# Batch 0's attention in products of 512 columns, with E and F loaded as 128 rows and the first half of k loaded uncast

## The chip, the cores and the metric

The kernel runs on one core of one Trainium2 chip. The metric is the device time of one execution in microseconds (us), the median over runs. The kernel before has 320.8 us (three runs, 320.7 to 321.04).

## The reference

Eight batches of attention with projected keys and values feed a maxout layer and an output product:

```python
k_proj = einsum('ks,bhsd->bhkd', E, k)          # E, F: 64 x 1024
v_proj = einsum('ks,bhsd->bhkd', F, v)          # q, k, v: 8 batches x 8 heads x 1024 x 64
attn = softmax(q @ k_proj^T / 8)                # 1024 x 64 for each head
x = (attn @ v_proj), heads side by side         # 8192 x 512
out = maximum(x @ w1, x @ w2) @ w_out           # 512 -> 1024 -> 512
```

Inputs and output are float32; the kernel computes in float16 with float32 accumulation.

## The kernel before

Every step is a Python function that issues instructions, and the order of the calls is the order on each engine: the schedule is written out by hand. Names in the profile are tile names; `step_...` are the functions.

The kernel has a short opening stage (0 to about 27 us) and a long steady stage. The opening stage loads and computes the attention of batch 0 and starts its first layer; the steady stage interleaves the attention of batch b + 1 with the two layers of batch b.

**Loads.** Three loads go on the SP queue: E (64 rows of 1024 float32), the first two heads of k as float32 (`kf_sb`, cast later by ScalarE and VectorE), and F. All others go on the POOL queue and are cast to float16 on the way: k heads 2 and 3; q heads 0 to 3; k heads 4 to 7; q heads 4 to 7; v in four pairs of heads; then the weights, in pieces. The first four pieces of the weights are the first 256 columns of w2 and w1: rows "g = 0" of w2, of w1, rows "g = 1" of w2, of w1. In what follows the fourth is called w1g1; POOL issues it at 16.04 us. From the ninth load of the POOL queue on, each waits until the one eight places earlier has landed.

**Attention of batch 0.** It goes in two groups of four heads (g = 0, 1) and, within a group, two halves of 256 query columns each (j = 0, 1).

- `step_eft(i)` transposes E and F by float32 transposes (L161); one copy evacuates each (L167).
- `step_kv(..., "k")` projects k for four heads (L187), `step_kpt` transposes the result (L277), `step_qt` transposes q (L303).
- `step_sc(g, j)` makes the scores (L332: tiles of 64 rows by 32 columns, 256 columns of q) and ScalarE takes the exponential (L372). `step_dn` sums by a product with ones (L344) and takes the logarithm (L380), `step_inv` the exponential of its negative (L384), that is the reciprocal.
- `step_kv(..., "v")` projects v, once for each half of the partitions, since the values are wanted on both.
- `step_at(g, j)` multiplies with the values (L344), and VectorE scales with the reciprocal into `xt_sb` (L399), two instructions for each (g, j), one for each output half o.

**First layer of batch 0.** `step_wd(f0, r0, r1)` (L495, VectorE) forms `wd = w1 - w2` for 256 columns and the row blocks r0 to r1. `up_slots` (L479) multiplies `xt` with `wd`, four row blocks r for each output block. The first four output blocks, two of each j, take r = 0, 1 as soon as group 0 is done, and r = 2, 3 when group 1 is. `step_w2t(f0)` (L504) transposes w2 for a later use. With its second argument it takes a buffer of the ring `att`.

**PSUM.** `mm_bank()` gives one of four banks in the order of the list `turn`; `att_banks()` gives the next of a ring of two buffers of two banks. A new user of a buffer waits for the last reader of the old one. Fillers, `warm(n)` (L147), are products of ones that nobody reads.

The end of the opening stage, as the calls are written:

```python
    step_kv(t, 4, 8, "v", True, copy=nc.scalar.copy)
    step_at(t, 1, 0, True)
    u0, u1 = [*up_slots(t, 0)], [*up_slots(t, 1)]
    step_wd(0, 2, 4)
    step_at(t, 1, 1, True)
    for u in u0, u1:
        for x in u[0:2]:
            x(r1=2)
    step_w2t(0, True)
```

After this come, for TensorE, `u0[0]` and `u0[1]` with r = 2, 3, `step_w2t(256, True)`, `u1[0]` and `u1[1]` with r = 2, 3, and the rest of the layer. The buffers of the ring `att` there: `step_at(1, 0)` has one, `step_at(1, 1)` the other, `step_w2t(0)` the first of the two again, `step_w2t(256)` the second.

Of the kernel before, what the change touches and what calls it, by code (L numbers as in the profile page):

```python
# [16 lines left out]
def kernel(  # L17
# [55 lines left out]
    def big(n, dtype=FP16):  # L73
        return const.tile([128, 16384 // mybir.dt.size(dtype) // 2], dtype, tag=f"big{n}", name=f"big{n}")

    ef_sb = big(0, FP32)[0:KP, :].rearrange("k (i s) -> k i s", i=2)
    kf_sb = const.tile([128, 2048], FP32, tag="wo", name="kf_sb")[:, 0 : 2 * NC * D].rearrange(
        "p (h c d) -> p h c d", h=2, d=D
    )
    nc.sync.dma_start(out=ef_sb[:, 0, :], in_=E)  # L80
    nc.sync.dma_start(out=kf_sb, in_=k[0, 0:2].rearrange("h (p c) d -> p h c d", c=NC))
    nc.sync.dma_start(out=ef_sb[:, 1, :], in_=F)
# [27 lines left out]
    for h0 in (0, H // 2):  # L110
        for n, src in (("k", k), ("q", q)):
            load(tiles[0], n, src, 0, h0 + 2 * ((h0, n) == (0, "k")), h0 + H // 2)
            if (h0, n) == (0, "k"):
                ident = const.tile([128, 128], FP32)
                make_identity(nc, ident)
# [24 lines left out]
    nc.vector.memset(ones16, 1.0)  # L140
    junk = const.tile([1, 1], FP16)


    def warm(n, att=False):
        w_ps = att_banks()[:, 0, :] if att else mm_bank()
        for _ in range(n):
            nc.tensor.matmul(  # L147
                out=w_ps, lhsT=ones16[:, 0:128], rhs=ones16, start=True, stop=True
            )

    warm(8)
    ident16 = const.tile([128, 128], FP16)
    nc.vector.tensor_copy(out=ident16, in_=ident)


    eft = [const.tile([128, NC, KP], FP16, tag=f"eft{i}", name=f"eft{i}") for i in range(2)]

    def step_eft(i):
        eft_ps = mm_bank()
        for c in range(NC):  # L160
            nc.tensor.transpose(  # L161
                out=eft_ps[:, c * KP : (c + 1) * KP],
                in_=ef_sb[:, i].rearrange("k (p c) -> k c p", c=NC)[:, c, :],
                identity=ident[:KP, :KP],
            )
        eng = nc.scalar.copy if i else nc.vector.tensor_copy
        eng(out=eft[i].rearrange("p c k -> p (c k)"), in_=eft_ps)  # L167
# [9 lines left out]
    def step_kv(t, h0=0, h1=H, which="kv", att=False, dma=False, copy=nc.vector.tensor_copy):  # L177
        kv_ps = att_banks()[:, 0, :] if att else mm_bank(n=0 if dma else None)
        n = (h1 - h0) * D
        both = which == "v"  # L180
        nh = 2 if both else h1 - h0
        for h in range(0, h1 - h0, nh):
            for c in range(NC):
                for w in which:
                    i = "kv".index(w)
                    for r in range(2) if both else (i,):
                        nc.tensor.matmul(  # L187
                            out=kv_ps[r * KP : (r + 1) * KP, h * D : (h + nh) * D],
                            lhsT=eft[i][:, c, :],
                            rhs=t[w][:, h0 + h : h0 + h + nh, c, :],  # L190
                            start=(c == 0), stop=(c == NC - 1),
                        )
        zd = lambda ap: ap.rearrange("p (h d z) -> p h z d", d=D // 2, z=2)
        if "k" in which:
            eng = nc.vector.tensor_copy if which == "k" or dma else nc.scalar.copy
            kp = t["kp"][:, h0:h1]
            eng(out=kp[:, :, 0, :], in_=kv_ps[0:KP, 0:n].rearrange("p (h d) -> p h d", d=D))
        if both:
            copy(out=t["vp"][:, h0:h1], in_=zd(kv_ps[:, 0:n]))
        elif "v" in which:  # L200
            def finish_v():
                nc.vector.tensor_copy(out=t["vp"][KP:128, h0:h1], in_=zd(kv_ps[KP:128, 0:n]))
                if dma:
                    nc.vector.tensor_copy(out=kp[:, :, 1, :], in_=kp[:, :, 0, :])
                    step_kpt_dma(t)
                else:
                    step_vp(t, h0, h1)

            if att:
                return finish_v  # L210
            finish_v()
# [59 lines left out]


    def step_kpt(t, h0=0, h1=H, att=False):
        kpt_ps = att_banks(FP16)[:, 0, :] if att else mm_bank(FP16)
        for h in range(h0, h1):
            for r in range(2):
                nc.tensor.transpose(  # L277
                    out=kpt_ps[r * D : (r + 1) * D, (h - h0) * KP : (h - h0 + 1) * KP],
                    in_=t["kp"][:, h, 0, :],
                    identity=ident16[:KP, :KP],  # L280
                )
        nc.vector.tensor_copy(
            out=t["kpt"][:, h0:h1, :].rearrange("q h k -> q (h k)"),
            in_=kpt_ps[:, 0 : (h1 - h0) * KP],
        )
# [100 lines left out]
    def step_at(t, g, j, att=False, between=None):  # L386
# [9 lines left out]
        for o in range(2):  # L396
# [7 lines left out]
            )  # L404

# [121 lines left out]
    T_sb = const.tile([128, 4, NG + NX, CH], FP16)  # L527
# [35 lines left out]
    def m_steps():  # L563
# [41 lines left out]
        def p5():  # L605
            st["s5"] = keep("pu", product(5, "Z", 3))
# [333 lines left out]
    for u in u0, u1:  # L940
        for x in u[0:2]:
            x(r1=2)
# [203 lines left out]
```

## Time and profile before

| | |
|---|---|
| median of the runs | 320.8 us |
| time of the profiled execution | 321.09 us |
| its span, first to last instruction | 319.3 us |
| TensorE (PE) busy | 312.9 us, 98% |
| VectorE (DVE) busy | 241.3 us, 76% |
| ScalarE (ACT) busy | 205.8 us, 64% |
| GpSimd (POOL) busy | 39.7 us, 12% |
| granted TensorE clock | 1.000 |

Busy time is a sum over instructions; a busy engine can still be at half its rate. Rows of the timeline read: start, busy time, engine, line, operation, output from input, shape, number of instructions, and the idle time before with what ended it. Rows of the table by stage read: the stretch, its length, busy time (and instructions) of PE, its weight loads, DVE, ACT and POOL, the granted clock, the busy share of the 16 DMA engines and the bytes that they wrote, in GB/s. A load that casts writes half of what it reads.

### The profile page before, as it was taken

The page shows a single profiled execution, that of the slowest core. Times are in us where ns is not written, and L with a number is a line of the kernel's source. Part 1 is how long each engine was busy: PE and PEld are TensorE (multiplying, and loading weights), DVE is VectorE, ACT ScalarE, POOL GpSimd, SP SyncE. Part 2 cuts the span into 40 slices and gives each one's busy share as a digit, 9 for nine tenths or more (in the row PEclk, how much of TensorE's full clock was granted, in tenths as well). Part 3 has the DMA queues.
Part 4 walks back from the last instruction along what each step waited for, and adds up shares of the span by engine and source line. Part 5 has one row for each costly group of instructions (what it writes and reads, how often), then busy time and mean ns, then how long its engine had stood idle before and what let it go on. Part 6 is the DMA issues. An engine that isn't in the chain of part 4 may idle for free.

```text
span 319.3 us, 9176 instructions
## 1 busy us (share of the span) xinstructions
PE 312.9 (98%) x3920; PEld 253.2 (79%) x3920; DVE 241.3 (76%) x434; ACT 205.8 (64%) x372; POOL 39.7 (12%) x63
## 2 busy tenths in 40 slices
PE   8989999999999999999999999999999999999996
PEld 3554588788887888788887888788887888888885
DVE  2356889787969696896969696996969696969683
ACT  2376742767776777477776777477776777765541
POOL 8269102003000300021000400030000000000000
PEclk9999999999999999999999999999999999999999
DMA  7999999999979899899999999889969231303124
GB/s 185 200 200 193 199 207 202 207 165 154 206 136 179 156 205 245 219 192 158 233 204 215 168 216 245 198 157 169 239 141 211 50 102 35 101 33 102 35 99 131
DMA packets 76424, 53.41 MB, mean 167 GB/s; under 512 B 29536, under 2 KB 76000, under 8 KB 76384
## 3 DMA queue, kind: packets, MB, share of 16 engines
q0 software_dynamic: 30688, 28.05, 56.2%
q1 hardware_dynamic: 45408, 24.58, 32.3%
q8 instruction: 30, 0.49, 0.6%
q10 hardware_dynamic: 288, 0.20, 0.2%
q14 instruction: 10, 0.08, 0.1%
HBM read 57.15 MB, written 16.78 MB: 232 GB/s over the span
## 4 chain that ended last, share of the span: by engine, by line
PE 92%; DMA 4%; ACT 1%; POOL 1%; DVE 1%; issue 0%; POOLq 0%; DVEq 0%
PE mm_ps L785 46%; PE mm_ps L693 27%; PE mm_ps L479 4%; DMA v_sb<-in_v_dram 4%; PE att_ps L344 3%; PE mm_ps L187 3%; PE mm_ps L332 3%; PE mm_ps L581 2%; PE att_ps L229 1%; PE mm_ps L303 1%; POOL k_sb L102 0%; POOL q_sb L102 0%; PE att_ps L504 0%; PE att_ps L332 0%; ACT ld_sb L384 0%
## 5 line engine op out<-in xcount | busy, mean ns | idle before, releaser
L667 ACT COPY p_sb<-mm_ps 128x512 f32<-128x512 f32 x179 | 101.7, 592 | 49.4 <-PE mm_ps L693 27.3
L785 PEld LDWEIGHTS <-big 128*128 128x128 f16 x768 | 73.5, 98 | 11.8 <-issue 3.6
L785 PE MATMUL mm_ps<-T_sb,big 128*128 128x256 f16 x576 | 77.0, 273 | 0.0
L708 DVE TENSOR_TENSOR gt_sb<-mm_ps,p_sb 128x512 f16<-128x512 f32 x56 | 38.5, 687 | 42.7 <-PE mm_ps L693 42.3
L693 PE MATMUL mm_ps<-big,big 128*128 128x256 f16 x336 | 50.4, 273 | 0.0
L693 PEld LDWEIGHTS <-big 128*128 128x128 f16 x448 | 43.8, 98 | 5.1
L785 PE MATMUL mm_ps<-wo_sb,gt_sb 128*128 128x256 f16 x256 | 42.8, 273 | 0.0
L785 PEld LDWEIGHTS <-gt_sb 128*128 128x128 f16 x376 | 35.6, 98 | 7.0 <-issue 3.0
L425 ACT ACTIVATE ex_sb<-mm_ps 128x512 f16<-128x512 f32 x50 | 27.2, 596 | 18.2 <-PE mm_ps L332 13.0
L693 PEld LDWEIGHTS <-wd_sb 128*128 128x128 f16 x336 | 32.9, 98 | 4.1
L693 PE MATMUL mm_ps<-xt_sb,wd_sb 128*128 128x256 f16 x224 | 33.0, 272 | 0.0
L454 DVE TENSOR_TENSOR xt_sb<-att_ps,ld_sb 128x1024 f16<-128x1024 f32 x26 | 31.7, 1218 | 0.2
L785 PE MATMUL mm_ps<-m_sb,xt_sb 128*128 128x256 f16 x128 | 24.4, 273 | 0.0
L711 DVE TENSOR_SCALAR gt_sb<-gt_sb 128x512 f16<-128x512 f16 (+1 forms) x60 | 22.7, 378 | 2.1
L815 DVE TENSOR_TENSOR o_sb<-mm_ps,p_sb 128x512 f32<-128x512 f32 x32 | 21.8, 682 | 2.8 <-ACT p_sb L839 2.0
L295 POOL COPY junk<-qt_sb 1x1 f16<-1x1 f16 x6 | 1.1, 177 | 176.2 <-DMA qt_sb<-q_sb 176.2
L653 DVE TENSOR_TENSOR big<-gt_sb 128x1024 f16<-128x1024 f16 x32 | 21.9, 683 | 0.0
L785 PE MATMUL mm_ps<-wo_sb,big 128*128 128x256 f16 x128 | 21.5, 273 | 0.0
L754 ACT ACTIVATE gt_sb<-mm_ps 128x512 f16<-128x512 f32 x28 | 16.8, 601 | 5.7 <-PE mm_ps L693 5.7
L785 PE MATMUL mm_ps<-T_sb,gt_sb 128*128 128x256 f16 x120 | 20.3, 273 | 0.0
L785 PEld LDWEIGHTS <-xt_sb 128*128 128x128 f16 x188 | 18.4, 98 | 2.1
L708 DVE TENSOR_TENSOR gt_sb<-p_sb 128x512 f16<-128x512 f32 x28 | 19.1, 682 | 0.7 <-ACT p_sb L667 0.6
(112 smaller groups left out, 434.7 us busy)
## 6 DMA issues: line engine op xcount, KB each, us to landing
out_dram<-o_sb SPq DMA_DIRECT2D x62, 256.0 KB, 2.7
k_sb<-in_k_dram POOLq DMA_DIRECT2D x7, 1024.0 KB, 10.4
v_sb<-in_v_dram POOLq DMA_DIRECT2D x7, 1024.0 KB, 17.0
q_sb<-in_q_dram POOLq DMA_DIRECT2D x5, 1024.0 KB, 23.9
q_sb<-in_q_dram POOLq DMA_DIRECT2D x6, 512.0 KB, 16.2
big<-in_moe_w_dram POOLq DMA_DIRECT2D x12, 128.0 KB, 6.3
v_sb<-in_v_dram POOLq DMA_DIRECT2D x4, 256.0 KB, 13.8
wo_sb<-in_moe_w_out_dram POOLq DMA_DIRECT2D x1, 1024.0 KB, 10.4
```

The source lines that it names most:

```text
L187: nc.tensor.matmul(out=kv_ps[r * KP : (r + 1) * KP, h * D : (h + nh) * D], lhsT=eft[i][:, c, :], rhs=t[w][:, h0 + h : h0 + h + nh, c, :], ...
L425: nc.scalar.activation(out=t["ex", g, j][:, e, :], in_=banks[e], func=ACTF.Exp, scale=scale)
L454: nc.vector.tensor_tensor(out=x_out(t, g, j).rearrange("q z o n -> q o z n"), in0=at_ps.rearrange("q o (z n) -> q o z n", z=2), in1=ld[:, ...
L479: nc.tensor.matmul(out=h_ps, lhsT=wd_sb[:, r, fb * 128 : (fb + 1) * 128], rhs=t["xt"][:, r, :, j * W : (j + 1) * W], start=(r == 0), stop= ...
L653: nc.vector.tensor_tensor(out=S(i), in0=S(0) if x is None else x, in1=y(), op=op)
L667: copy(out=x, in_=bank)
L693: nc.tensor.matmul(out=bank[:, m * W : (m + 1) * W], lhsT=w_[:, n_, (2 * d + m) * 128 : (2 * d + m + 1) * 128], rhs=a[:, n_, :], start=(n ...
L708: nc.vector.tensor_tensor(out=c_blk(j, c), in0=two(x), in1=two(y), op=ALU.add)
L711: nc.vector.tensor_scalar_max(ap, ap, 0.0)
L754: nc.scalar.activation(out=out, in_=in_, func=ACTF.Relu)
L785: nc.tensor.matmul(out=bank[i][:, 0:CH] if two_banks else bank[:, i * CH : (i + 1) * CH], lhsT=a(c)[:, i * 128 : (i + 1) * 128], rhs=w_(c) ...
L815: nc.vector.tensor_tensor(out=o_sb, in0=two(x), in1=two(y), op=ALU.add)
```

## The change

- E and F are loaded as 128 rows of 512 (each row of 1024 in two halves); a copy makes them float16, and a product with a rearranged identity transposes them. F's transpose is kept twice side by side (`fdup`), so that one product projects v onto both halves of the partitions.
- k heads 0 and 1 (SP queue) and heads 2 and 3 (ACT queue) are both loaded as float32 and cast by VectorE and ScalarE. The POOL queue has one load fewer and begins with q.
- Scores, sums and values of batch 0 go over all 512 columns at once: `step_sc0`, `step_dn0`, `step_inv0`, `step_at0` (group 0, four banks of `mm_bank`) and `step_at1` (group 1, both buffers of `att`, one for each output half o).
- The calls are put in a new order. Among others, `step_wd(0, 2, 4)` stands before all scaling of group 1, and the sums of group 1 come after the values of group 0.
- The fillers are float32 and fewer; one product of the steady stage's start (`p5`) uses bank 1 where it used bank 3.

```diff
-    nc.sync.dma_start(out=ef_sb[:, 0, :], in_=E)
-    nc.sync.dma_start(out=kf_sb, in_=k[0, 0:2].rearrange("h (p c) d -> p h c d", c=NC))
-    nc.sync.dma_start(out=ef_sb[:, 1, :], in_=F)
+    halves = lambda w: w.rearrange("k (h s) -> (k h) s", h=2)
+    nc.sync.dma_start(out=ef_sb[:, 0], in_=halves(E))
+    for n, queue in enumerate((nc.sync, nc.scalar)):
+        queue.dma_start(
+            out=raw_sb[:, n], in_=k[0, 2 * n : 2 * n + 2].rearrange("h (p c) d -> p h c d", c=NC)
+        )
+    nc.sync.dma_start(out=ef_sb[:, 1], in_=halves(F))
...
-    for h0 in (0, H // 2):
-        for n, src in (("k", k), ("q", q)):
-            load(tiles[0], n, src, 0, h0 + 2 * ((h0, n) == (0, "k")), h0 + H // 2)
...
+    load(tiles[0], "q", q, 0, 0, H // 2)
+    ident16 = const.tile([128, 128], FP16)
+    make_identity(nc, ident16)
+    for n, src in (("k", k), ("q", q)):
+        load(tiles[0], n, src, 0, H // 2, H)
...
     def step_eft(i):
+        ps_t = att_banks().rearrange("p b (c h k) -> p (b c) h k", h=2, k=KP)
         for c in range(NC):
+            nc.tensor.matmul(
+                out=ps_t[0:KP, c],
+                lhsT=ef16[:, i].rearrange("q (p c) -> q c p", c=NC)[:, c, :],
+                rhs=ident16.rearrange("q (k h) -> q h k", h=2),
+                start=True, stop=True,
             )
+        for h in range(2):
+            rows, src = slice(h * KP, (h + 1) * KP), ps_t[0:KP, :, h, :]
+            if i == 0:
+                (nc.scalar.copy if h else nc.vector.tensor_copy)(out=eft[0][rows], in_=src)
+            else:
+                nc.scalar.copy(out=fdup[rows], in_=src[:, :, None, :].broadcast_to([KP, NC, 2, KP]))
+        if i:
+            nc.vector.tensor_copy(out=eft[1], in_=fdup[:, :, 0, :])
...
+    def step_at1(t):
+        at_ps = [att_banks() for _ in range(2)]
+        for z in range(2):
+            tiles0(t, 1, lambda o: at_ps[o][:, z, :], lambda rows, hh: vp_of(t, 4 + hh, rows, z))
+        for j in range(2):
+            for o in range(2):
+                cols = slice(j * W, (j + 1) * W)
+                nc.vector.tensor_tensor(
+                    out=t["xt"][:, 2:4, o, cols], in0=at_ps[o][:, :, cols],
+                    in1=ld0[:, 1, o, None, cols].broadcast_to([128, 2, W]), op=ALU.mult,
+                )
...
-            st["s5"] = keep("pu", product(5, "Z", 3))
+            st["s5"] = keep("pu", product(5, "Z", 1))
...
+    nc.vector.tensor_copy(out=ef16[:, 0], in_=ef_sb[:, 0])
+    cast = lambda eng, h: eng(out=t["k"][:, h], in_=raw_sb[:, h // 2, h % 2])
+    cast(nc.vector.tensor_copy, 2)
+    cast(nc.scalar.copy, 3)
     step_eft(0)
+    cast(nc.vector.tensor_copy, 0)
+    cast(nc.scalar.copy, 1)
+    nc.scalar.copy(out=ef16[:, 1], in_=ef_sb[:, 1])
+    warm(512, 256)
+    step_k0(t, 0, 4)
+    warm(256)
+    step_kpt0(t, 0, 4)
     step_eft(1)
+    warm(256)
+    step_qt(t, 0)
+    step_qt(t, 2)
+    step_sc0(t, 0)
+    step_k0(t, 4, 8)
+    step_dn0(t, 0)
+    step_inv0(0)
+    step_kpt0(t, 4, 8)
+    warm(256)
+    step_qt(t, 4)
+    step_qt(t, 6)
+    step_sc0(t, 1)
+    step_v0(t, 0, 4, 4, nc.vector.tensor_copy)
+    step_at0(t, lambda: step_wd(0, 0, 2))
+    step_dn0(t, 1)
+    step_v0(t, 4, 8, 2, nc.scalar.copy)
+    step_inv0(1)
     u0, u1 = [*up_slots(t, 0)], [*up_slots(t, 1)]
     step_wd(0, 2, 4)
-    step_at(t, 1, 1, True)
-    for u in u0, u1:
-        for x in u[0:2]:
-            x(r1=2)
+    step_at1(t)
+    turn.sort(key=(2, 3, 1, 0).index)
+    for r in range(2):
+        for u in u0, u1:
+            for x in u[0:2]:
+                x(r0=r, r1=r + 1)
     step_w2t(0, True)
```

The lines taken out of the old order (the calls of `step_kv`, `step_kpt`, `step_sc`, `step_dn`, `step_inv`, `step_at` and the float16 `warm` for batch 0) are left out here, as are the new functions `step_k0`, `step_kpt0`, `step_v0`, `step_sc0`, `tiles0`, `step_dn0`, `step_inv0` and `step_at0`, whose work is named above.

## The prediction

> **What bounds the kernel now.** First the head of the page: span and busy time. Then the chain that ended last, from 0 to 60 us, for the place where the opening stage hands over to TensorE.
>
> ```profile
> span 319.3 us, 9176 instructions
> PE 312.9 (98%) x3920; PEld 253.2 (79%) x3920; DVE 241.3 (76%) x434; ACT 205.8 (64%) x372; POOL 39.7 (12%) x63
> ...
> 4.84 13.53 DMA v_sb<-in_v_dram
> ...
> 23.49 1.90 PE mm_ps L479 x8
> 25.38 0.59 PE att_ps L504 x8
> 25.98 0.88 PE mm_ps L479 x4
> 26.86 0.04 issue
> 26.90 0.61 PE att_ps L504 x8
> 27.51 4.32 PE mm_ps L479 x20
> ```
>
> The chain leaves the DMA with v at 18.37 us and stays on PE from 23.49 on. From there PE works without a gap to the end (the table by ten microseconds shows it busy 10.00 of 10.00 nearly throughout), and the change leaves its work behind the opening stage as it is. So the time changes by exactly as much as the stretch after the first eight products (L479) shifts: I follow the first L504, which started at 25.34 (timeline), and what stands behind it. Nothing won before that row counts if it starts no sooner.
>
> What could hold it there is VectorE. The timeline of DVE from 17 to 28 us:
>
> ```profile
> 21.20 1.89 DVE L399 TENSOR_TENSOR xt_sb<-mm_ps,ld_sb 128x512 f16<-128x512 f32 x3 [0.91 <-PE mm_ps L344]
> 23.01 0.42 DVE L495 TENSOR_TENSOR wd_sb<-big,big 128x512 f16<-128x512 f16 x1
> 23.34 0.69 DVE L399 TENSOR_TENSOR xt_sb<-mm_ps,ld_sb 128x512 f16<-128x512 f32 x1
> 23.94 1.28 DVE L399 TENSOR_TENSOR xt_sb<-att_ps,ld_sb 128x512 f16<-128x512 f32 x2
> 25.14 0.42 DVE L495 TENSOR_TENSOR wd_sb<-big,big 128x512 f16<-128x512 f16 x1
> 25.47 1.28 DVE L399 TENSOR_TENSOR xt_sb<-att_ps,ld_sb 128x512 f16<-128x512 f32 x2
> ```
>
> The fourth row ends at 25.22 and frees the first of the two `att` buffers: L504 starts 0.12 us later. The second L495 forms rows r = 2, 3 of wd and needs the fourth weight piece, w1g1, issued at 16.04. The DMA answer for that issue, and the table by stage of the first microseconds:
>
> ```profile
> big<-in_moe_w_dram POOLq DMA_DIRECT2D x1, 128.0 KB, 8.9
> ```
>
> ```profile
> 2.00:3.00 1.00, 1.00 (x4) 0.32 (x3) 0.23 (x1) 0.03 (x1) 0.92 (x4) 1.00 0.80 193
> 3.00:4.00 1.00, 1.00 (x4) 0.30 (x3) 0.00 (x0) 0.00 (x0) 1.00 (x2) 1.00 0.98 258
> 7.00:8.00 1.00, 0.99 (x9) 0.72 (x8) 0.23 (x1) 0.00 (x0) 1.00 (x2) 1.00 1.05 155
> 13.00:14.00 1.00, 1.00 (x22) 0.48 (x7) 0.00 (x0) 1.00 (x2) 0.50 (x1) 1.00 1.24 207
> ```
>
> w1g1 landed at 16.04 + 8.9 = 24.94. Before, L495 took it at 25.14 and nobody noticed, for two scalings of group 1 stood ahead of it. From about 8 us to 60 us the DMA engines write some 200 GB/s, that is read 400, without a pause: w1g1 comes when the bytes ahead of it are through.
>
> **The change part by part.**
>
> *Half the instructions on TensorE.* Group 1's values were 32 products of 256 columns (L344, busy 0.63); now 16 of 512, the same columns. Between 0.32 (half) and 0.63; I take 0.45. The same holds for scores and sums, whose rows stand among fillers and waits. None of it is on the path at the end, since PE will wait for VectorE there; if it did not, all that is left is 0.2 us.
>
> *k and E, F.* The bytes that the DMA engines read up to w1g1 are the same, since k's heads 2 and 3 only go uncast; what can change is how full the engines are at the start. From 2 to 8 us they wrote 193 + 258 + 335 + 204 + 339 + 155 = 1484 GB/s x 1 us, 1.48 MB in all. The three plain loads are 1.05 MB of it; the other 0.43 MB were cast, so 0.87 read: 1.92 MB. At the later 405 GB/s that is 4.7 of the 6 us. So 0 to 1.3 us can be won for all later loads. Two queues and POOL's one load fewer (its first took 0.83 us of issue) fill the start, but the ramp at 2 us stays: I take the middle, 0.6. w1g1 then lands at 24.3 (23.6 to 24.9).
>
> The Trainium skill speaks against this gain: "DMA: Bandwidth & Descriptors", section "Issuing engines are not separate DMA queues", says that issuing from more engines saves only the issue time, as all run on the same 16 DMA engines. By it the gain would be an issue at most, and the sum below stays within its ends.
>
> *F's new path.* F is cast on ACT (L902's 0.6), transposed, copied twice on ACT (128x1024 from PSUM, L510: 1.02 each) and then once on DVE, ahead of q's copies, which ran at 11.41 and now come near 12.7. Group 0's scores are later by 1.3; what hides it is v, landing at 18.35 and 19.2 (pairs 1 and 2). Without that cover it costs 1.3.
>
> *Values of group 0.* They now need both first pairs of v: 19.2 - 0.6 = 18.6. Eight products of 256 columns (1.0, L187), the copy (0.42), half the values (0.3), 0.2 of hand-overs: the first scaling at about 20.5 instead of 21.20.
>
> *The order on DVE.* This is what I take to decide. The engine runs in order: four scalings of group 0 with the first L495 between, then `step_wd(0, 2, 4)`, then all four scalings of group 1. Behind the wait for w1g1 stand all of these. And each `att` buffer of `step_at1` now holds one output half for both column halves, so that the first buffer is free for `step_w2t(0)` after the third scaling (j = 1, o = 0), not after the second. PE, also in order, has `step_w2t(0)` ahead of the r = 2, 3 products. By the DVE rows: group 0's four scalings and the first L495 end near 20.5 + 4 x 0.61 + 0.35 = 23.3. Then DVE waits. Start of the second L495 24.3 + 0.1, its length to the next start 0.33 (25.14 to 25.47), three scalings 3 x 0.61 + 0.05 = 1.9, hand-over 0.12: L504 starts at 26.8 instead of 25.34, **1.45 us later**. PE, which will be done with its eight products at about 24.6, waits 2.1 us. What is late next, the second L504 and the fourth scaling, comes 0.6 later, when PE is still at the four products (0.88): no further wait. `step_inv0(1)` (two rows of L384, 1.14) ends near 23.3 and is hidden by the wait for w1g1.
>
> *The rest.* The casts of k, the float32 fillers, bank 1 for `p5` (PE has no gap at L581) have v's landing or a busy PE over them: nothing; without that cover some tenths.
>
> The sum is made against the profiled execution: 321.09 + 1.4 = 322.5. The median of the runs, 320.8, is 0.3 below it, so 322.2. With the DMA gain at its ends, 1.3 and 0: plus 0.75 to 2.05, that is 321.55 to 322.85.
>
> **The rivals.**
>
> *Weights early (faster).* By 24.94 the engines had written 1.48 + 17 x 0.2 = 4.9 MB, while all loads up to w1g1 make 1.05 + 3.41 = 4.46: the landing waits for a straggler, 2.1 us behind the mean. If loads over all 128 rows remove that lag as well, w1g1 comes up to 3.4 us earlier and DVE alone decides: from the first scaling to the end of the third of group 1 seven scalings and two L495, 7 x 0.61 + 2 x 0.35 = 5.0, where there were 4.02. The first scaling would come at about 19.5, after group 1's scores, so L504 0.7 us earlier: 320.1. It decides from a landing before 22.3 on. For it: v's second pair would gain too. Against: v and the weights come on POOL's queue as before, and nothing shows that E's 64 rows make the straggler.
>
> *Both halfway (no change).* w1g1 at 22.3 to 23.5: within 0.6 us of before, about 321.0.
>
> *A cold TensorE (slower still).* The first eight fillers took 3.60 us, 0.45 each, the next five 1.25, 0.25 each: PE begins at half rate. If the waits near 12 and 24 us bring that back, the eight products of L479 (1.90) take 3.6: 323.9. Against: the fillers stay between the waits. "TensorE: Matmul & The Clock Gate", part 1, puts the relapse after an idle window of some 3.4 us, longer than my gaps.
>
> **How the numbers follow.** A measurement can tell about 0.2%, 0.64 us. Forecast (order on DVE) 0.60; cold TensorE 0.06; no change 0.17; weights early 0.17. Slower 0.66, same 0.17, faster 0.17. The range leaves out most of the early-weights case and the top of the cold one: 320.3 to 323.2; the forecast's own is 321.55 to 322.85.
>
> **What would show it.** Right: DVE idle by more than 0.5 us before the second `step_wd`, ended by the weight DMA; PE idle 1.5 to 2.5 us before the first product of `step_w2t(0)`, ended by the scaling of group 1; w1g1 landing near 24.3; from there the same chain, shifted. Wrong: w1g1 landing before 23, or that L504 starting before 25.34. The F path is wrong as told if q's copies come before 12 us, and the cover is gone if v's first products wait for anything but v.

## The result, and the profile after

The changed kernel takes 323.22 us (median of 8 runs, 322.67 to 324.88) against 320.82 us before: the ratio is 1.0083, with an interval from 1.006 to 1.0106. It is slower, as forecast, but by 2.4 us and not by 1.4, just above the range. The profiled execution took 322.67 us, the shortest of the eight; its span is 320.9 us, 1.6 above that of before.

The head of the page:

```profile
span 320.9 us, 8861 instructions
PE 311.0 (97%) x3764; PEld 253.4 (79%) x3764; DVE 242.2 (75%) x436; ACT 208.8 (65%) x372; POOL 38.8 (12%) x62
```

TensorE has 156 instructions and 1.9 us of work fewer, and the span is longer: a stage that is no longer filled with TensorE's work. The chain that ended last, from 0 to 60 us, says where (columns: start, length, what):

```profile
6.11 0.69 DVE eft L175
...
6.83 0.58 ACT eft L175
...
7.43 0.63 ACT k_sb L987
...
8.10 1.05 PE mm_ps L216 x8
...
11.33 1.01 ACT fdup_sb L177
...
12.35 1.01 ACT fdup_sb L177
...
13.39 0.38 DVE eft L179
13.76 0.60 DVE qt_sb L328
...
14.41 0.43 PE att_ps L436 x4
...
14.87 1.95 ACT ex_sb L443 x2
...
19.93 0.41 PE att_ps L436 x4
20.34 0.99 PE mm_ps L240 x8
...
22.40 0.70 DVE xt_sb L476
...
26.80 0.69 DVE xt_sb L487
...
27.63 0.61 PE att_ps L590 x8
```

Before, this chain left the DMA with v at 18.37 and was on TensorE from 23.49 on. Now no transfer is in it after the start: it runs from the copies of E's transposes (L175) and k's cast (7.43), which stands behind them on ScalarE, through k's first products (8.10, where before they ran at 7.28), F's transposes, both of F's copies on ScalarE, VectorE's copy of F (L179), q's copies (L328), both groups of scores, v's first products (L240 at 20.34) and the scalings (L476, L487), and it reaches TensorE's first product of `step_w2t(0)` (L590) at 27.63, where the chain of before has L504 at 25.38: 2.25 us later. (The prediction's 25.34 is the weight load that belongs to it.) The timeline of VectorE from 19.5 us on:

```profile
22.40 1.89 DVE L476 TENSOR_TENSOR xt_sb<-mm_ps,ld_sb 128x512 f16<-128x512 f32 x3 [0.61 <-PE mm_ps L453]
24.20 0.41 DVE L581 TENSOR_TENSOR wd_sb<-big,big 128x512 f16<-128x512 f16 x1
24.53 0.68 DVE L476 TENSOR_TENSOR xt_sb<-mm_ps,ld_sb 128x512 f16<-128x512 f32 x1
25.14 0.41 DVE L581 TENSOR_TENSOR wd_sb<-big,big 128x512 f16<-128x512 f16 x1
25.59 2.48 DVE L487 TENSOR_TENSOR xt_sb<-att_ps,ld_sb 128x512 f16<-128x512 f32 x4
```

The second L581 is `step_wd(0, 2, 4)`. It has no idle time before it, so nobody waited for w1g1. The DMA answer for that piece, issued at 15.51, gives its landing: 15.51 + 8.3 = 23.81, where before it was 24.94. One profile says little of a landing, though: worked out in the same way, it is 24.3 in the three other profiles with the loads of before (runs 8, 9 and 12 below), and 23.7 to 24.7, 24.0 in the mean, in the eleven with the new loads (this one and runs 1 to 3, 6, 7, 10, 11 and 13 to 15).

```profile
big<-in_moe_w_dram POOLq DMA_DIRECT2D x1, 128.0 KB, 8.3
```

The stretch that decides lies earlier, in the timeline of VectorE and of TensorE from 10 to 15 us:

```profile
13.39 0.38 DVE L179 COPY eft<-fdup_sb 128x512 f16<-128x512 f16 x1 [2.86 <-ACT fdup_sb L177]
13.69 1.27 DVE L328 COPY qt_sb<-mm_ps 128x1024 f16<-128x1024 f16 x2
14.41 0.41 PE L436 MATMUL att_ps<-qt_sb,kpt_sb 64*64 64x512 f16 x4 [1.59 <-DVE qt_sb L328]
```

q's transposes were done at 12.8; VectorE stood idle for 2.86 us at the head of its queue, because L179, which waits for ScalarE's second copy of F, is ahead of q's copies. The copies ran at 13.69 (before: 11.41), and TensorE waited 1.59 us for them.

Part of the 2.25 us comes back behind L590. From its start to the start of the 20 products of L565 it is 1.91 us, where before it was 2.13: there the second group of L504 took 0.61 us after a pause of 0.04, here 0.45 without one. L667's 56 products take 6.11 where L581's took 6.25. What is left of the way down to the 1.6 us of the span, some 0.3, comes back between 48 us and the end, and how stays open.

### The profile page after: what moved, and what is told of

Read it like the earlier page. It is cut to its first block, busy times and chain, and to the rows that moved or that the text cites. A ratio compares the mean times of both kernels' runs of the same rounds, so it can differ in the third digit from the quotient of the medians.

```text
span 320.9 us, 8861 instructions
## 1 busy us (share of the span) xinstructions
PE 311.0 (97%) x3764; PEld 253.4 (79%) x3764; DVE 242.2 (75%) x436; ACT 208.8 (65%) x372; POOL 38.8 (12%) x62
## 4 chain that ended last, share of the span: by engine, by line
PE 94%; DVE 3%; ACT 2%; issue 1%; DVEq 0%
PE mm_ps L871 46%; PE mm_ps L779 27%; PE mm_ps L565 4%; PE att_ps L364 3%; PE mm_ps L194 3%; PE mm_ps L352 2%; PE mm_ps L667 2%; PE att_ps L264 1%; PE mm_ps L152 1%; PE att_ps L166 1%; PE mm_ps L323 1%; PE mm_ps L240 1%; ACT fdup_sb L177 1%; ACT ex_sb L443 1%; DVE qt_sb L328 1%
## 5 line engine op out<-in xcount | busy, mean ns | idle before, releaser
L511 ACT ACTIVATE ex_sb<-mm_ps 128x512 f16<-128x512 f32 x50 | 27.2, 596 | 18.0 <-PE mm_ps L352 12.8
L797 DVE TENSOR_SCALAR gt_sb<-gt_sb 128x512 f16<-128x512 f16 (+1 forms) x60 | 21.7, 362 | 2.1
L840 ACT ACTIVATE gt_sb<-mm_ps 128x512 f16<-128x512 f32 x28 | 16.8, 601 | 5.7 <-PE mm_ps L779 5.7
## 6 DMA issues: line engine op xcount, KB each, us to landing
q_sb<-in_q_dram POOLq DMA_DIRECT2D x6, 512.0 KB, 13.2
```

What stands on the lines that cost most here:

```text
L511: nc.scalar.activation(out=t["ex", g, j][:, e, :], in_=banks[e], func=ACTF.Exp, scale=scale)
L797: nc.vector.tensor_scalar_max(ap, ap, 0.0)
L840: nc.scalar.activation(out=out, in_=in_, func=ACTF.Relu)
```

## The experiments

One theory of the chain of waits ("the chain is late, and three things make it so: F's path, the order of the scalings, a TensorE that starts slowly") stands against the prediction's theory ("the weights' landing holds VectorE"). Each run has its own runs of the kernel before, whose medians lie between 320.85 and 320.95.

**1. F's copy moved behind q's copies.**

```diff
-        if i:
-            nc.vector.tensor_copy(out=eft[1], in_=fdup[:, :, 0, :])
...
     step_sc0(t, 0)
+    nc.vector.tensor_copy(out=eft[1], in_=fdup[:, :, 0, :])
     step_k0(t, 4, 8)
```

> The kernel after, with one instruction moved: VectorE's copy of F's transpose for the later batches (eft[1], which batch 0 does not use) stands behind both copies of q's first half instead of ahead of them. Theory 'chain' (batch 0's attention itself is late: q's copies waited until 13.69 us for ScalarE's two fdup copies, so scores, exponentials, v's product and the first scaling all came late): q's copies start near 12.3, the first exponential at 13.4 (when ScalarE is through with fdup), 1.4 us earlier than 14.87; the first scaling comes 1 to 1.5 earlier than 22.40 and the first product of step_w2t(0) 1 to 1.4 earlier than 27.63; the time falls by 1.0 to 1.5 us, to about 1.0 above the kernel before. Theory 'weights' (the landing of the fourth weight piece and the order behind it decide): w1g1 still lands near 23.8, VectorE reaches it no later than in the kernel after, and the time stays within 0.3 us.

322.7 us (321.43 to 323.38); ratio 1.0041, interval 1.001 to 1.0071. Two of six executions gain over 1 us on the shortest of the changed kernel, the others at most 0.3. In the profiled one, among the others, k's first products start at 9.18 instead of 8.10, because the fillers ahead of them took 2.93 us instead of 1.75 (below). Its wait on VectorE is gone, but the gain is eaten ahead of it. Taken alone it was no verdict.

**2. step_w2t(0) moved behind the four products of u0 with r = 2, 3.**

```diff
-    step_w2t(0, True)
...
-        (0, lambda: u0[0](r0=2)), (1, lambda: u0[1](r0=2)), (None, lambda: loads(1, "v", "q", "k")),
+        (0, lambda: u0[0](r0=2)), (1, lambda: u0[1](r0=2)), (None, lambda: step_w2t(0, True)),
+        (None, lambda: loads(1, "v", "q", "k")),
```

> The kernel after, with the first transposes of w2 (step_w2t(0), which waits for the third scaling of group 1) moved on TensorE behind the products of u0[0] and u0[1] with r = 2, 3, which need only two scalings. Theory 'order' (part of the loss is that the ring buffer of both column halves makes TensorE wait for one scaling more): those products start 0.6 us after the second scaling ends, near 26.95 instead of 28.07, the transposes follow without a wait; the time falls by 0.6 to 1.1 us. Rival (something later, such as the fourth scaling or the second transposes, holds TensorE instead): less than 0.3 us.

323.97 us, from 322.0 to 325.89; ratio 1.0087, interval 1.0045 to 1.013. The scatter hides what the move does. The profile shows what scatters: in the table by stage the granted clock is 0.83 from 10 to 20 us, after TensorE idled from 13.2 to 14.7:

```profile
10.00:20.00 10.00, 8.05 (x73) 5.65 (x73) 2.97 (x7) 6.03 (x6) 4.00 (x6) 0.83 1.24 205
```

In that stretch eight products of k (L216) took 1.44 us instead of 1.06. The rows by the microsecond, with the granted clock third from the end, show when:

```profile
16.00:17.00 1.00, 1.00 (x8) 0.56 (x5) 0.00 (x0) 1.00 (x2) 0.37 (x1) 0.58 1.23 205
17.00:18.00 1.00, 0.91 (x13) 0.37 (x12) 0.68 (x1) 0.29 (x2) 0.70 (x1) 0.50 1.25 206
18.00:19.00 1.00, 1.00 (x6) 0.72 (x5) 0.29 (x1) 0.97 (x2) 0.70 (x1) 0.50 1.23 203
19.00:20.00 1.00, 1.00 (x13) 0.82 (x12) 0.00 (x0) 0.91 (x1) 0.49 (x2) 0.71 1.26 199
```

If the clock is either 1.00 or 0.50, this is one lapse of (0.42 + 0.50 + 0.50 + 0.29) / 0.5 = 3.4 us (an estimate from these rows). It is the prediction's rival "cold TensorE", in three of the six executions by their mean clock (0.995, 0.989 and 0.989). A fourth, 324.45, is as long without it.

**3. One more filler in the gap before the first scores.**

```diff
     step_qt(t, 2)
+    warm(512, 256, n=turn[0])
     step_sc0(t, 0)
```

> The kernel after, with one more filler (768 float32 columns, about 1.3 us at full rate) in TensorE's gap between q's transposes and the first scores (12.8 to 14.4 us). Theory 'clock' (the spread of the kernel after, 322.7 to 324.9, is TensorE falling to half rate in some executions, whose mean granted clock is 0.989 to 0.994): the executions draw together at 322.5 to 323.1 with a mean clock of 0.999 to 1.000, median 0.3 to 0.7 lower. Rival (the spread has another source, such as the loads): spread and median stay. In both the best execution stays at 322.7.

323.17 us (322.62 to 324.83); ratio 1.0072, interval 1.004 to 1.0105: no gain. With the gap at 13 us filled, all six executions have a granted clock of 0.999 or 1.000, as the theory said, and yet they scatter by 2.2 us, as the rival said: it is not the lapses of the clock alone that make the scatter. The profiled execution, 324.59, again has its second fillers at 2.93 us, k's first products at 9.19 and the first L590 at 29.52.

**4. Early loads in the kernel before.** k's heads 2 and 3 go uncast on ScalarE's queue, POOL has one load fewer and starts with q; E and F stay as 64 rows.

```diff
+    for n, queue in enumerate((nc.sync, nc.scalar)):
+        queue.dma_start(
+            out=raw_sb[:, n], in_=k[0, 2 * n : 2 * n + 2].rearrange("h (p c) d -> p h c d", c=NC)
+        )
```

> The kernel before, with one part of the change alone: k's heads 2 and 3 uncast on the ACT queue (and cast by VectorE and ScalarE), POOL's queue one load shorter and beginning with q; E and F stay 64 rows. Theory 'queues' (the earlier landings of the kernel after come from this): v's first pair lands near 16.6 instead of 18.35, the fourth weight piece near 23.8 instead of 24.94. Rival 'rows' (they come from E and F over all 128 rows): v lands within 0.4 us of 18.35. The time: the opening stage before waited for v at 18.4, so with v early it falls by 0.2 to 0.6 us; if scores and scalings bound it by then, 0 to 0.2.

322.41 us (321.31 to 322.79); ratio 1.0035, interval 1.0007 to 1.0063: slower. v is early, as in the changed kernel: POOL's issue that waits for v's first pair ran at 16.80 (before 18.66, after 16.87). So an early v does not need E and F as 128 rows, and by itself it buys nothing. How much of it comes from the queues is less clear: with all the loads of before this issue ran at 17.36, 17.00 and 17.42 in runs 8, 9 and 12, so that most of the 1.8 us belongs to the one profile of before; and in run 5, with the loads of this run, it ran at 17.85. E now lands at 5.9 us (0.74 + 5.2) instead of 4.7, TensorE idles for 0.98 us, falls behind, and q's copies run at 13.24.

**5. The same, with k's load behind ScalarE's table load.** Only the order of ScalarE's first two instructions is changed, which was meant to put E ahead.

```diff
-    for n, queue in enumerate((nc.sync, nc.scalar)):
-        queue.dma_start(...)
     nc.scalar.add_instruction(
         mybir.InstLoadActFuncSet(...)
     )
+    for n, queue in enumerate((nc.sync, nc.scalar)):
+        queue.dma_start(...)
```

> The kernel before with k's heads 2 and 3 uncast on ScalarE's queue, but issued behind ScalarE's table load of 1.3 us, so that E lands first. Theory "early v is worth time where E is not delayed": E lands at 4.9 to 5.2 us (5.90 with the load ahead of the table load), k's first products at 7.3 to 7.8 us, v's first pair by 17 us, step_w2t(0) at 24.3 to 25.3 (25.34 in the kernel before); median 319.6 to 320.8. Rival "v's landing is not what the chain waits for": v lands early and the median stays at 320.7 to 321.5, or above it where k's products come late.

322.24 us (321.29 to 323.63); ratio 1.0035, interval 1.0022 to 1.0048. It failed, and it tests nothing: ScalarE's queue issued k's load at 0.77 us, where in run 4 it was 0.74, so E was no further ahead than there. E landed at 6.1 us (0.74 + 5.4) and k's first products ran at 10.03. What delays E here is not settled; E as 128 rows, in the changed kernel, had landed at 4.1 in spite of the same loads on the same two queues.

**6. float16 fillers.** Seven, five and two products of 512 columns, as in the kernel before, and no second memset ahead of them, so that they start at 1.46 instead of 2.00.

```diff
-    warm(512, 256)
+    warm(*[512] * 7)
...
-    warm(512, 256)
+    warm(*[512] * 5)
     step_k0(t, 0, 4)
-    warm(256)
+    warm(512, 512)
```

> The changed kernel with float16 fillers of 512 columns in place of the float32 ones: seven before E's products, starting right after the first memset, five before k's first products, two in the later gaps. Theory "the chain is late because TensorE is still at half rate when E's and k's products run": E's 8 products take under 1 us (1.22 before this edit), the five fillers about 1.25 us, k's first products start at 7.0 to 7.7 us (8.10), the scores, the first scaling (22.40) and the first product of step_w2t(0) (27.63) come 0.4 to 1 us earlier; median 321.9 to 322.6. Rival "F's path alone sets the chain": q's copies stay at 13.7 and the median at 323.0 to 323.4.

322.56 us (322.44 to 322.99); ratio 1.0052, interval 1.004 to 1.0064. The scatter is smaller (0.55 us over five executions, where it was 2.2 over eight), and the median is 0.66 lower than the changed kernel's 323.22. But k's products came only at 7.98, so that the theory's mechanism, an earlier start of k's products by 0.4 to 1.1 us, is not what is seen; q's copies stay at 13.63, still behind F.

**7. float16 fillers, and F's copy moved.** Edits 6 and 1 together.

> The run with float16 fillers, with VectorE's copy of F's transposes also moved behind q's copies and the first scores. Theory "F's path held q's copies back": q's copies run at 11.3 to 12 us (13.69), the first scaling at 20.2 to 21.2 (22.40), step_w2t(0) at 25.2 to 26.3 (27.63), median 320.3 to 321.6, so 1 to 2 us under the run with the fillers alone. Rival "v or a weight piece sets the end, as the prediction had it": q's copies move, but the first scaling or the second group stays within 0.5 us of 22.4 or 27.6 and the median within 0.5 us of the run with the fillers alone.

321.44 us (321.13 to 322.03); ratio 1.0017, interval 1.0009 to 1.0025. F's copy on VectorE is worth 322.56 - 321.44 = 1.12 us, in a comparison without the scatter. VectorE's timeline has q's copies ended by q's transposes now, not by F:

```profile
13.09 1.29 DVE L324 COPY qt_sb<-mm_ps 128x1024 f16<-128x1024 f16 x2 [1.79 <-PE mm_ps L319]
```

The time of 13.09 is late because in this execution E landed half a microsecond later and the second fillers took 2.31 us; it was the longest of the twelve. Even so `step_w2t(0)` came at 26.96, 0.67 earlier than in the changed kernel.

**8. The 512-column attention with the loads of the kernel before.** E and F as 64 rows with float32 transposes, k's heads 2 and 3 cast on POOL's queue, float16 fillers, F's second copy by ScalarE from `eft[1]`. Of the kernel before's `step_eft`:

```diff
         eng = nc.scalar.copy if i else nc.vector.tensor_copy
         eng(out=eft[i].rearrange("p c k -> p (c k)"), in_=eft_ps)
+        if i:
+            nc.scalar.copy(out=fdup, in_=eft[1][:, :, None, :].broadcast_to([128, NC, 2, KP]))
```

> The 512-column attention of batch 0 alone: the loads of the kernel before (E and F as 64 rows through float32 transposes, k's heads 2 and 3 cast on the gpsimd queue, eight float16 fillers first); F's second copy is made by ScalarE from eft[1]. Theory "the attention itself is worth its saving and the new load and transpose path is what comes late": k's first products at 7.2 to 7.5 us, q's copies at 11.4 to 12, v's products at 18.5 to 19.5, the first scaling at 20.5 to 21.3, step_w2t(0) at 25.3 to 26.3; median 319.8 to 321.2. Rival "the 512-column form itself makes the chain longer": q's copies at 11.4 to 12, but the first scaling still at 21.5 or later and the median at 321.5 to 323.

322.07 us (321.56 to 323.1); ratio 1.0036, interval 1.0024 to 1.0049. Each expectation came true by half: the first scaling is where the theory had it, the median where the rival had it. This is the prediction's mechanism as it was told. q's copies ran at 12.29 and the first scaling at 20.92, 0.28 earlier than before, and still the handover is late. VectorE and TensorE, from 23 us:

```profile
24.39 0.42 DVE L572 TENSOR_TENSOR wd_sb<-big,big 128x512 f16<-128x512 f16 x1 [0.33 <-DMA big<-in_moe_w_dram]
24.74 2.48 DVE L478 TENSOR_TENSOR xt_sb<-att_ps,ld_sb 128x512 f16<-128x512 f32 x4
...
26.76 0.61 PE L581 MATMUL att_ps<-ident,big 128*128 128x128 f16 x8 [0.98 <-DVE xt_sb L478]
```

The second `step_wd` waits for w1g1, the four scalings stand behind it, and TensorE waits 0.98 us for the third of them.

**9. The same with step_w2t(0) moved**, with the diff of run 2, to test that.

> The 512-column attention with the loads of the kernel before, with step_w2t(0) moved behind the four products of u0 with r 2 and 3, which wait for two scalings of group 1 where step_w2t(0) waits for three. Theory "what the 512-column form costs is the wait for the third scaling": TensorE's wait of 0.98 us before step_w2t(0) falls to 0.2 to 0.4 us, step_w2t(0) runs without one, median 321.2 to 321.6 (322.07 without the move). Rival "the cost lies earlier, in the chain up to the first up products": median within 0.3 us of 322.07.

321.21 us (320.92 to 321.38); ratio 1.0006, interval 0.9997 to 1.0014: 0.86 us won, as the theory has it. TensorE waits 0.31 us, for the second scaling, and `step_w2t(0)` not at all.

**10. Edits 6, 1 and 2 together:** the changed kernel with float16 fillers, F's copy moved and `step_w2t(0)` moved.

> The run with float16 fillers and F's copy moved, with step_w2t(0) behind the four products of u0 with r 2 and 3. Theory "third scaling": the wait of 0.51 us before step_w2t(0) goes, median 320.8 to 321.1 (321.44 without the move). Rival "the wait is made up for later on a full TensorE, or comes back before the Relus of u0": median within 0.2 us of 321.44.

320.86 us (320.57 to 321.08); ratio 0.9996, interval 0.9988 to 1.0005. The wait for the third scaling was worth 321.44 - 320.86 = 0.58 us. TensorE goes through its twelve products and the transposes without a gap, and q's copies run at 12.24, 1.4 us earlier than in the changed kernel. VectorE still waits 0.22 us for w1g1:

```profile
12.24 1.29 DVE L324 COPY qt_sb<-mm_ps 128x1024 f16<-128x1024 f16 x2 [1.79 <-PE mm_ps L319]
...
23.93 0.42 DVE L577 TENSOR_TENSOR wd_sb<-big,big 128x512 f16<-128x512 f16 x1 [0.22 <-DMA big<-in_moe_w_dram]
```

TensorE from 23.7 us:

```profile
23.71 2.92 PE L561 MATMUL mm_ps<-xt_sb,wd_sb 128*128 128x512 f16 x12
26.47 1.06 PE L586 MATMUL att_ps<-ident,big 128*128 128x128 f16 x16
```

With this the whole loss is undone: three edits of order and filler, and the changed loads and attention are level with the kernel before.

**11. The chain made shorter still.** Edits 1, 2 and 6, and in addition:

```diff
     step_eft(1)
-    warm(512, 512)
     step_qt(t, 0)
...
+    step_qt(t, 4)
     step_dn0(t, 0)
     step_inv0(0)
     step_kpt0(t, 4, 8)
-    warm(512, 512)
-    step_qt(t, 4)
     step_qt(t, 6)
-    step_sc0(t, 1)
-    step_v0(t, 0, 4, 4, nc.vector.tensor_copy)
+    step_sc0(t, 1, lambda: step_v0(t, 0, 4, 4, nc.vector.tensor_copy))
```

> The run with float16 fillers and F's copy moved, with three more changes of order: step_w2t(0) behind the four products of u0 with r 2 and 3, q's transposes of heads 4 to 7 split around the first denominators with the fillers before both groups of q's transposes dropped, and v's first products between the two halves of group 1's scores. Theory "the time is set by one chain from k's products to group 1's scalings, until TensorE is full at about 27 us": q's first copies 0.4 us earlier, v's first products 0.8 to 1.2 us earlier (19.60 in the run it is built on), first scaling at 20.4 to 21 (21.73), the first product of the up step at 23.3 to 23.9 (24.54), no wait of TensorE over 0.3 us behind it; median 319.6 to 320.4. Rival "v's or the weights' landing takes over": the first scaling is at 20.4 to 21, the second subtraction or the scalings of group 1 wait for a transfer, and the median stays at 320.8 or above.

320.83 us (320.57 to 321.27); ratio 0.9998, interval 0.9989 to 1.0006: no faster than run 10, though the first scaling came at 20.28. The rival holds: v (TensorE waits 0.64 us for it at 18.17) and then the weights take over. VectorE from 22 us:

```profile
22.66 0.43 DVE L579 TENSOR_TENSOR wd_sb<-big,big 128x512 f16<-128x512 f16 x1 [0.49 <-DMA big<-in_moe_w_dram]
...
24.08 0.42 DVE L579 TENSOR_TENSOR wd_sb<-big,big 128x512 f16<-128x512 f16 x1 [0.40 <-DMA big<-in_moe_w_dram]
```

Both subtractions now wait for a weight piece. This shortening of the chain won nothing, and no version ran that beats both kernels.

**12. The changed kernel's float32 fillers in the kernel before.** Nothing else changed but these and the second memset.

```diff
+    ones32 = opool.tile([128, 512], FP32, tag="o", name="ones32_sb")
+    nc.vector.memset(ones32, 1.0)
...
-        for _ in range(n):
+        for m in (512, 256) if n > 3 else (256,):
             nc.tensor.matmul(
-                out=w_ps, lhsT=ones16[:, 0:128], rhs=ones16, start=True, stop=True
+                out=w_ps[:, 0:m], lhsT=ones32[:, 0:128], rhs=ones32[:, 0:m], start=True, stop=True
             )
```

> The kernel before with the changed kernel's float32 fillers (512 and 256 columns where there were eight and five products, 256 where there were two or three), nothing else changed. Theory "the kind of filler sets when TensorE comes to full rate, and so part of the changed kernel's loss and all of its scatter": executions spread over 1 to 3 us where those of the kernel before lie within 1, the second filler group takes 1.75 or 2.93 us, median 321.2 to 322.5. Rival "the fillers are all alike": median within 0.3 us of 320.9 and no more scatter than the kernel before.

321.85 us (320.85 to 322.58, where the kernel before had 320.53 to 321.4); ratio 1.0028, interval 1.0015 to 1.0041. So in these rounds the edit costs time and brings scatter. Why, it does not show: kind, number and start of the fillers change together, and run 8, with float16 fillers, scatters by 1.5 us as well. The profiled execution does not point to the fillers: its second fillers took 1.56 us, at full rate, and k's first products, at 8.66, waited for k's heads on POOL's queue. That transfer landed 5.8 us after its issue in the profile of before, and 6.8 to 7.3 us after it in three runs with the same loads (8, 9 and this one).

**13 to 15. Kind or start of the fillers.** Run 10 with the float32 fillers; with float16 fillers behind a second memset (from 2.00 us, six instead of seven); and with float32 fillers whose memset comes first (from 1.46 us, 64 columns more). The first has the diffs of runs 1 and 2 alone. Against run 10, the second has:

```diff
+    ones32 = opool.tile([128, 512], FP32, tag="o", name="ones32_sb")
+    nc.vector.memset(ones32, 1.0)
     ones16 = const.tile([128, 512], FP16)
     nc.vector.memset(ones16, 1.0)
...
-    warm(*[512] * 7)
+    warm(*[512] * 6)
```

Against the first of these runs, the third has:

```diff
+    ones32 = opool.tile([128, 512], FP32, tag="o", name="ones32_sb")
+    nc.vector.memset(ones32, 1.0)
     ones16 = const.tile([128, 512], FP16)
     nc.vector.memset(ones16, 1.0)
-    ones32 = opool.tile([128, 512], FP32, tag="o", name="ones32_sb")
-    nc.vector.memset(ones32, 1.0)
...
-    warm(512, 256)
+    warm(512, 320)
```

> The changed kernel with F's copy behind the first scores and step_w2t(0) behind u0, with its own float32 fillers. Theory "the fillers are worth the remaining 0.7 us and the scatter": median 321.3 to 322.2, executions spread over 1 us or more, where the same kernel with float16 fillers gave 320.86 within 0.5. Rival "the fillers only cost where F's path is in the way": median 320.7 to 321.1 and little scatter.

> The run with float16 fillers, F's copy and step_w2t(0) moved, with a second memset ahead of the fillers and six in place of seven first ones, so that they start at 2.0 us and not at 1.46. Theory "start": the later start of a busy TensorE brings the loss, median 321.3 to 322.2 and more scatter. Theory "kind": median within 0.2 us of 320.86.

> The run with float32 fillers, with their memset first, so that they start at 1.5 us, and 64 columns more in the first group so that they last until E is there. Theory "start": median 320.7 to 321.1 and executions within 0.6 us. Theory "kind": as in the run with float32 fillers from 2.0 us, 321.3 to 322.2, scattered.

321.08 us (320.7 to 321.88), 321.13 us (320.52 to 322.0) and 321.38 us (320.66 to 322.89); ratios 1.0004, 1.0002 and 1.0015, with intervals of some 0.0014 on either side. All three scatter, and in these rounds the kernel before did too (320.48 to 322.87), so neither theory is shown. The medians are 0.2 to 0.5 us above that of run 10, which is of other rounds, and the intervals overlap with its own: with F and the third scaling out of the way no cost of the fillers is shown.

## Why the prediction was right and wrong

The direction was right, and the step it rested on exists; but in the changed kernel another step came first, and that is the one that was mis-sized.

| kernel | median | lowest | undone |
|---|---|---|---|
| changed | 323.22 | 322.67 | |
| run 6 | 322.56 | 322.44 | fillers: 0.66 in the median, 0.23 in the lowest |
| run 7 | 321.44 | 321.13 | F's copy on VectorE: 1.12, 1.31 |
| run 10 | 320.86 | 320.57 | third scaling: 0.58, 0.56 |

The three make 2.36 us of the 2.40; that they add up is no proof, since run 10 is level with the kernel before and each row is a difference to the next. The medians are of different rounds, so the last digits are not worth much; the intervals of the ratios of runs 6 and 7, and of 7 and 10, do not meet, while those of the changed kernel and of run 6 do by a little: the fillers' share is the least certain of the three, and how they act is not shown.

*F's new path: the step that failed.* The prediction found the copy ahead of q's copies, and held that it makes group 0's scores later by 1.3 us, that v's landing hides this, and that "without that cover it costs 1.3". The cover did not hold. v's first products (L240) ran at 20.27, directly behind the second group's scores and without a wait for v: in TensorE's order they stand behind both groups of scores, and so behind q's copies and F. So the first scaling was not at 20.5 but at 22.40. The text had named this sign itself ("the cover is gone if v's first products wait for anything but v"). I had counted the product from v's landing alone and never followed the other chain, from k and F through the scores, up to the same product; the maximum of the two was wanted. From the first scores to v's first products it is 20.27 - 14.41 = 5.86 us, so even scores that are late by 1.3 alone would have put v's products at about 12.19 + 1.3 + 5.86 = 19.35 (an estimate), behind the 18.6 of the prediction.

The scores came 2.2 us later (14.41 against 12.19), and this is two terms. F's copy is the larger: in run 10, which does without it on the path, q's copies run 1.4 us earlier than in the changed kernel (12.24 against 13.69). The price of 1.3 was about right; run 7 measures 1.12 in the median. The other 0.8 was there before F: k's first products ran at 8.10 instead of 7.28, held by ScalarE's cast of k, which stands behind its copy of E's transposes. Run 10 still has it (8.02). The prediction had put the casts of k at "nothing", "without that cover some tenths".

*The loads.* "The middle, 0.6" was about right, and w1g1's landing at 24.3 too: the eleven profiles with the new loads have 24.0 in the mean, the four with those of before 24.5. The 1.13 us between the profiles of before and after is mostly the late landing in the former. It is the same with v, on whose landing the cover rested: its first pair released POOL's waiting issue at 18.66 in that profile, at 17.0 to 17.4 in the three others with the same loads, and at 16.8 to 17.2 with the new ones. The prediction had read both landings from one execution. The rule of the Trainium skill ("DMA: Bandwidth & Descriptors", section "Issuing engines are not separate DMA queues") would have limited the gain to an issue, 0.83 us, and these means, some 0.5 us earlier for w1g1 and 0.6 for v, do not contradict it. The prediction's own count of bytes agrees: from 1 to 8 us the engines now wrote 41 + 166 + 324 + 404 + 399 + 268 + 233 = 1835 GB/s x 1 us, that is 1.84 MB, 1.57 of it by the four plain loads, so that 2.10 MB were read instead of 1.92; the 0.18 MB are 0.44 us at 405 GB/s (an estimate). In time, run 9 against run 10, whose intervals overlap, gives 321.21 - 320.86 = 0.35 us for the new loads together with the new transposes of E and F.

*The order on VectorE.* Right as a mechanism, in the kernels in which it can show. Run 8 has the wait for w1g1, the scalings behind it and TensorE's wait for the third one, at 0.98 us instead of 2.1, since in it the first scaling came at 20.92 and the first products ran later. In the changed kernel VectorE reached its second `step_wd` only at 25.14, when w1g1 had landed, and would have been later than the 24.94 of before as well. So of this step only the third scaling was left: a wait of 0.51 us before L590, worth 0.58 in run 10. I had L504 at 26.8 and TensorE idle for 2.1 us there; it was 27.63 and 0.51.

*Half the instructions on TensorE.* Priced at 0.2 us at most, and it is less than can be told: run 9, the new attention with the old loads and without the wait, is at 321.21, not below the kernel before. The 16 products of 512 columns still take 0.63 us (L453), as the 32 of 256 did: my 0.45 was wrong and cost nothing.

*The rest, and the cold TensorE.* The float32 fillers, too, had "nothing; without that cover some tenths": there was no cover, and taking them out gave 0.66 in the changed kernel (run 6), with a cause that stays open; the casts of k are told above. The rival "cold TensorE" had 0.06. It isn't what separates the medians: the five executions of the changed kernel with a granted clock of 0.999 or 1.000 have a median of 323.0. But it is there in executions: the three longest, 324.40 to 324.88, have granted clocks of 0.994 and 0.989, run 2 shows such a stretch, and one execution of the kernel before, in the rounds of runs 1 to 4, took 323.93 at 0.989. Its place in run 2 is not 24 us but 16 to 20 us, behind the gap that F's path makes. The prediction had set the rival aside because its gaps were shorter than the idle window that it quotes; in run 2 the clock fell after an idle time of 1.51 us (13.18 to 14.69), so that reason did not hold.

*The sum.* The span grew by 1.6 us, close to the 1.4 of the forecast, and that is luck: the first scaling came 1.9 us later than forecast (22.40 against 20.5), and from there to `step_w2t(0)` it took 5.2 us instead of 6.3, since the wait for w1g1 was missing. On the median of before the 1.6 would give 322.4. The other 0.8 lies in the profiled executions: that of before was 0.3 us above its median, that of after, the shortest of eight, 0.55 below.

## What to carry to other kernels

When a step is called hidden by a transfer, follow the other chain to the same instruction through every in-order queue, and take the later of the two; and ask whether the same change moves the cover. A copy that only a later use needs belongs behind the copies that the path needs, on an engine that runs in order: one 0.4 us copy at the wrong place cost 1.1 us. And read a landing from more than one execution: here the profile of before had v and the fourth weight piece 0.6 us or more later than three others with the same loads, and the profile of after was the shortest of executions that scattered by 2.2 us.

## What the runs showed of the hardware

Granted clock and rate are not the same at the start. The table by stage shows 1.00 in every one of the first stretches, and yet the same second group of fillers, two float32 products of 512 and 256 columns, took 1.75 us in the changed kernel and 2.93 in runs 1 and 3. TensorE's timelines of the changed kernel and of run 1 (the first row of each is E's transposes, the second the fillers):

```profile
4.86 1.22 PE L166 MATMUL att_ps<-ident,ef_sb 128*64 128x128 f16 x8
6.00 1.75 PE L152 MATMUL mm_ps<-ones_sb 128*128 128x512 f32 x4
```

```profile
5.17 1.22 PE L166 MATMUL att_ps<-ident,ef_sb 128*64 128x128 f16 x8 [0.24 <-DVE ef_sb L984]
6.32 2.93 PE L152 MATMUL mm_ps<-ones_sb 128*128 128x512 f32 x4
```

Here TensorE had idled for 0.24 us before E's transposes, and k's products behind the fillers were slow too (1.46 us in run 1, 1.92 in run 3, 1.03 in the changed kernel). But the length of this idle time does not sort the executions. Run 2 idled longer and had the full rate:

```profile
5.26 1.17 PE L166 MATMUL att_ps<-ident,ef_sb 128*64 128x128 f16 x8 [0.33 <-DVE ef_sb L986]
6.36 1.56 PE L152 MATMUL mm_ps<-ones_sb 128*128 128x512 f32 x4
```

With float32 fillers, idle times of 0, 0.22, 0.25 and 0.33 us went with 1.56 to 1.61 us (runs 12, 15, 13 and 2), 0 with 1.75 (the changed kernel), and 0.24 and 0.26 with 2.93 (runs 1 and 3). With five float16 fillers, no idle time went with 1.25 us (runs 8, 9, 14 and the kernel before), 0.04 to 0.15 us with 1.26 to 1.85 (runs 10, 6 and 11), and 0.55, 0.98 and 1.26 us (runs 7, 4 and 5) with 2.31, half the rate. So after half a microsecond of idling this early, all three profiles were slow; below that both were seen, and what decides is open. That this makes the scatter is argued and not shown: no single run was seen in both ways.

Later in a kernel the granted clock does show a loss of rate. In run 2 TensorE idled for 1.51 us up to 14.69; the clock was 1.00 up to 16 us and 0.50 from 17 to 19, and the eight products of k that began at 15.63 took 1.44 us instead of 1.06.
